# VectorE's two half steps of one tile, declared independent across its two PSUM banks

## The chip, the cores and the metric

One core of a Trainium2 chip runs the kernel. The metric is the time of one execution on the device, in microseconds; lower is better. The profiles are those of single executions, taken by the hardware profiler.

## What is computed

A channel attention feeds a rational feed-forward layer. The attention works on the 256 channels: its scores are 256 by 256 for each of the 4 batches, summed over 6080 rows.

```python
def _attn_ref(q, k, v, tau):                      # (4, 6080, 256) each
    qn = q / (np.linalg.norm(q, axis=1, keepdims=True) + 1e-06)
    kn = k / (np.linalg.norm(k, axis=1, keepdims=True) + 1e-06)
    s = kn.transpose(0, 2, 1) @ qn / tau
    a = softmax(s)                                # over the last axis
    return v @ a

def _moe_ref(x, w_in, w_out, a, b):               # x: (24320, 256), w_in: (256, 2048)
    h = x @ w_in
    P = a[0] + a[1] * h + a[2] * h * h + a[3] * h ** 3
    Q = 1.0 + abs(b[0]) * abs(h) + abs(b[1]) * h * h
    return (P / (Q + 1e-06)) @ w_out
```

## The kernel before

The softmax matrix of a batch is multiplied into w_in once (`fuse`, in 8 parts), so that the main work of a batch is two matmuls with the rational function between them. The 6080 rows of a batch are 12 groups, 11 of 512 rows and one of 448; a group has 8 pairs, each for 256 of the 2048 hidden channels. That makes 48 groups and 384 pairs. Every float32 operand of the large matmuls is held as a high and a low part in TensorE's faster float32 format, and three products stand for one.

What one pair does (`pair`, from line 842), on a PSUM tile `hx` of two banks, one for each 128 channels; x = 0 or 1 is the bank:

- TensorE: `mm1` (line 859), 12 matmuls, 6 into each bank. There are three `hx` tiles, so pair m + 3 needs each bank that pair m frees.
- ScalarE: five activations over both banks at once (lines 886 to 894 and 918): absolute value into `d`, a square into `uu`, a square on `d`, a reciprocal square root from `d` into `r`, and the square of `r`.
- VectorE: the numerator in place in `hx` (line 892), and the quotient's high part into `gh` (line 925), over both banks.
- GpSimd: `d` scaled (line 896), then `d` times the high part, for each bank alone (line 939).
- VectorE, for each bank alone: the remainder in place in `hx[:, x]` (line 941, "rest"), and its product with `r` into `gl[:, x]` (line 945, "last"), the low part of the quotient. In the profile they are `hx<-hx,fast,d` and `gl<-hx,r` of 128x512; the numerator is `hx<-uu,fast,hx`, the quotient `gh<-hx,fast,r`, both 128x1024. In this text: remainder 0 and 1, product 0 and 1.
- TensorE: `out_hi` (8 matmuls on `gh`) and `out_lo` (4 matmuls on `gl`) into the sum `acc` of the group.

Product x is the last reader of its bank, so it is what pair m + 3's matmuls into that bank wait for.

The order on each engine is not left to the compiler. `Planner.order` (line 178) works through all steps with costs and due times (the tables at lines 21 to 50) and gives one list; the steps are issued in that order. `InOrder` (line 69) wraps each engine: behind every instruction it calls `keep_in_program_order` (line 80), which ties the instruction to the one before it on the same engine, and then `apart`. The planner's plan is the same before and after the change.

The dependencies, and with them the waits on semaphores, are found by the framework from the tiles that instructions read and write. `hx` counts as one tile. `apart` (line 335) takes some of these dependencies back: `half[0]` holds, while a step runs, the slot and bank that it uses and its other buffers; `seen` keeps the last 40 instructions of each slot and bank; and `declare_no_dep` says that an instruction needs no dependency on one of another engine that used the other bank and none of the same buffers. Instructions of one and the same engine were left out of it.

The flag `quick` chooses at run time between two bodies of the program; the traces are of the first.

Of the kernel before, what the change touches and what calls it, by code (L numbers as in the profile page):

```python
# [125 lines left out]
def flat(bufs):  # L126
    return [x for b in bufs for x in (b.both if isinstance(b, Pair) else [b])]
# [165 lines left out]
def tile_channel_attention_rational_ffn(  # L293
# [38 lines left out]
    half = [None]  # L332
    seen = {}

    def apart(eng, ins):


        if half[0] is None:
            return
        slot, bank, rest = half[0]  # L340
        for other, old, used in seen.get((slot, 1 - bank), ()):
            if other is not eng and not used & rest:
                tc.declare_no_dep(ins.ins, old.ins, reason="the two use different banks of one tile")
        mine = seen.setdefault((slot, bank), [])
        mine.append((eng, ins, rest))
        del mine[:-40]

    pe = InOrder(tc, nc.tensor, apart)
    dve = InOrder(tc, nc.vector, apart)
    act = InOrder(tc, nc.scalar, apart)  # L350
    pool = InOrder(tc, nc.gpsimd)
    sp = InOrder(tc, nc.sync)
# [15 lines left out]
    def buf(tag, shape, dtype=F32, name=None):  # L368


        def view(slot):
            sizes = dict(zip("abc", shape[1:]))
            t = homes[tag][slot]
            if t.dtype != dtype:
                t = t.bitcast(dtype)
            t = t[:, : math.prod(shape[1:])]
            names = " ".join(sizes)
            return t.rearrange(f"p ({names}) -> p {names}", **sizes) if len(sizes) > 1 else t

        homes.setdefault(tag, 0)  # L380
        homes[tag] = max(homes[tag], math.prod(shape[1:]))
        return Buf(tag, view)
# [75 lines left out]
    def body(quick):  # L458
        lag, when = (LAG, TIME) if quick else (GENERAL_LAG, GENERAL_TIME)
        plan = planner(when)  # L460
        II, T0 = when["pair"], when["start"]
        def step(eng, cost, key, fn, reads=(), writes=(), port=False, rank=None):
            new = [b for b in flat(writes) if b.tag is not None and not b.writers]
            used = {id(b): b for b in (*flat(reads), *flat(writes))}.values()
            own = [b for b in used if b.tag in ("hA", "hB")]
            rest = [b for b in used if b.tag not in ("hA", "hB")]

            def run():
                for b in new:
                    b.tile = b.view(b.slot)  # L470
                at = {(b.slot, b.tag == "hB") for b in own}
                if len(at) == 1:
                    half[0] = *at.pop(), {(b.tag, b.slot) if b.tag else id(b) for b in rest}
                fn()
                half[0] = None

            plan.add(eng, cost, key, run, reads, writes, port, rank)
# [4 lines left out]
        def piece(side, m, at, c):  # L482
# [71 lines left out]
            else:  # L554
                dst, ok = None, w_out_ok[m]
                where = slice(2 * m, 2 * m + 2)
                whi, wlo = (x[:, where].rearrange("p f e -> p (f e)") for x in (w_out_hi, w_out_lo))
            step("SP", 1.45, at, load, (), [raw])
            step("ACT", 0.67, c, rescale, [raw], [kept])
            one, two = (0.45, 0.7) if port else (0.62, 0.7)  # L560
            step("DVE", one, c, low_bits, [kept], [work], port)
            step("DVE", two, c + 0.1, high_bits, [kept, work], [work], port)
            step("DVE", one, c + 0.2, power, [work], [work], port)
# [278 lines left out]
        def pair(m, at, vparts, w, acc):  # L842
# [3 lines left out]
            s = n / 512  # L846
            (vhi, vlo), (whi, wlo) = vparts, w
            hx = banks()
            d, r = buf("d", [P, 2, GT]), buf("r", [P, 2, GT])
            y = buf("uu", [P, 2, GT], F32, "uu")  # L850

            def c(b):
                return b[:, :, :n]

            def due(name):
                x = lag[name]
                return at + (x[p] if isinstance(x, tuple) else x)

            def mm1(i):
                idx = 0  # L860
                for e in range(NC2):
                    for a, x in ((whi, vhi), (whi, vlo), (wlo, vhi)):
                        pe.matmul(
                            hx[:, i, :n], a[:, e, i * P : (i + 1) * P], x[:, e, :n],
                            start=(idx == 0), stop=(idx == 3 * NC2 - 1),
                        )
                        idx += 1

            for i in range(2):
                fn = lambda i=i: mm1(i)  # L870
# [8 lines left out]
                                start=(first and i == parts[0] and a is w[0]), stop=(last and i == 1 and a is w[-1]),  # L879
                            )  # L880

            def put(eng, per, fixed, name, fn, reads, writes, rank=None, later=0.0):
                step(eng, per * s + fixed, due(name) + later, fn, reads, writes, False, None if rank is None else at + rank)

            if quick:
                fn = lambda: act.activation(c(d), c(hx), AF.Abs)
                put("ACT", 0.87, 0.16, "abs", fn, [hx], [d], 1.0)
                fn = lambda: act.activation(c(y), c(hx), AF.Square, bias=half2)
                put("ACT", 0.87, 0.25, "zz", fn, [hx], [y], 1.0)
                fn = lambda: act.activation(c(d), c(d), AF.Square, bias=half1)  # L890
                put("ACT", 0.87, 0.22, "shift", fn, [d], [d])
                fn = lambda: dve.scalar_tensor_tensor(c(hx), c(y), kappa, c(hx), op0=ALU.add, op1=ALU.mult)
                put("DVE", 1.06, 0.23, "num", fn, [y, hx], [hx])
                fn = lambda: act.activation(c(r), c(d), AF.Abs_reciprocal_sqrt, bias=eps)
                put("ACT", 0.87, 0.22, "root", fn, [d], [r], 6.0)
                fn = lambda: pool.tensor_scalar(c(d), c(d), ones[:, 0:1], eps, op0=ALU.mult, op1=ALU.add)
                put("POOL", 1.06, 0.1, "one", fn, [d], [d])
                first = c0
            else:
                kk = buf("uu", [P, 2, GT], F32, "kk")  # L900
                fn = lambda: act.activation(c(kk), c(hx), AF.Abs, scale=b1)
                put("ACT", 0.87, 0.25, "kk", fn, [hx], [kk], 1.0)
                fn = lambda: dve.scalar_tensor_tensor(c(d), c(kk), b0, c(hx), op0=ALU.add, op1=ALU.mult)
                put("DVE", 1.06, 0.22, "prod", fn, [kk, hx], [d], 1.0)
                fn = lambda: act.activation(c(d), c(d), AF.Abs)
                put("ACT", 0.87, 0.2, "absd", fn, [d], [d])
                fn = lambda: act.activation(c(y), c(hx), AF.Identity, scale=a3, bias=a2)
                put("ACT", 0.87, 0.33, "slope", fn, [hx], [y], 1.0)
                fn = lambda: dve.tensor_tensor(c(y), c(y), c(hx), op=ALU.mult)
                put("DVE", 1.06, 0.16, "num1", fn, [y, hx], [y])  # L910
                fn = lambda: dve.scalar_tensor_tensor(c(hx), c(y), a1, c(hx), op0=ALU.add, op1=ALU.mult)
                put("DVE", 1.06, 0.23, "num2", fn, [y, hx], [hx])
                fn = lambda: act.activation(c(r), c(d), AF.Abs_reciprocal_sqrt, bias=ONE)
                put("ACT", 0.87, 0.2, "root", fn, [d], [r], 6.0)
                fn = lambda: pool.tensor_scalar(c(d), c(d), ones[:, 0:1], ONE, op0=ALU.mult, op1=ALU.add)
                put("POOL", 1.06, 0.07, "one", fn, [d], [d])
                first = a0
            fn = lambda: act.activation(c(r), c(r), AF.Square)
# [3 lines left out]
            ghi, glo = buf("gh", [P, 2, GT], F32R), buf("gl", [P, 2, GT], F32R)  # L922
            ghi_ok = Buf()
            t_ok, glo_ok = ([Buf() for _ in range(2)] for _ in range(2))
            fn = lambda: dve.scalar_tensor_tensor(c(ghi), c(hx), first, c(r), op0=ALU.add, op1=ALU.mult)
# [11 lines left out]
            def tail(x):  # L937
                h = hx.both[x]
                fn = lambda: pool.tensor_tensor(d[:, x, :n], d[:, x, :n], ghi[:, x, :n].bitcast(F32), op=ALU.mult)
                put("POOL", 1.16, 0.1, "again", fn, [d, ghi, ghi_ok], [t_ok[x]], later=0.1 * x)  # L940
                fn = lambda: dve.scalar_tensor_tensor(
                    hx[:, x, :n], hx[:, x, :n], first, d[:, x, :n], op0=ALU.add, op1=ALU.subtract
                )
                put("DVE", 0.53, 0.22, "rest", fn, [h, d, t_ok[x]], [h], later=0.1 * x)
                fn = lambda: dve.tensor_tensor(glo[:, x, :n], hx[:, x, :n], r[:, x, :n], op=ALU.mult)
                put("DVE", 0.53, 0.14, "last", fn, [h, r, *([glo] if x else [])], [glo_ok[x], *([] if x else [glo])], 10.0, 0.1 * x)

            for x in range(2):
                tail(x)
                out_hi(x)  # L950
                out_lo(x)
# [70 lines left out]
        for G in range(TG):  # L1022
            b, g = divmod(G, NG)
            at = T0 + G * NFP * II
# [57 lines left out]
```

## Time and profile before

| | |
|---|---|
| median of 3 runs | 2478.53 us (2477.7 to 2479.44) |
| the profiled execution's own time | 2477.43 us |
| its span, first to last instruction | 2475.4 us |
| busy: TensorE, VectorE, ScalarE, GpSimd | 96%, 89%, 88%, 72% |
| granted TensorE clock, mean | 0.987 of full speed |

PE is TensorE (PEld its weight loads), DVE VectorE, ACT ScalarE, POOL GpSimd. Matmuls are pipelined and their ends are modelled: a row's duration reaches past the start of the next. In a timeline a row is: start, duration, engine, line, operation, what it writes and reads, shapes and count; behind it, in brackets, how long the engine had been idle before it and what released it. Neighbours of one kind stand as one row (x2). All instructions have line 79, that of the wrapper.

### The profile page before, as it was taken

Reading aid. Unit: us, or ns where it says so; the run is one execution under the profiler, and the core shown is the slowest. Engines: PE = TensorE matmul, PEld = TensorE weight load, DVE = VectorE, ACT = ScalarE, POOL = GpSimd, SP = SyncE. Lnnn points to the kernel's source line nnn. Section 1 sums busy time; section 2 is a strip of 40 time slices with the busy share of each in tenths; the row PEclk is TensorE's granted clock in tenths of the full one; section 3 lists DMA queues with packets and bytes.
Section 4 is the critical chain, followed back from the end, with each engine's and each line's share of the span. In section 5 each row is a group of like instructions: output and inputs, shape, how many; then the busy total and the mean of one; then the engine's idle time right before and its main releaser. Section 6 shows DMA issues by size and latency. Waiting matters only on the chain.

```text
span 2475.4 us, 30913 instructions
## 1 busy us (share of the span) xinstructions
PE 2375.3 (96%) x10400; PEld 1942.0 (78%) x10400; DVE 2196.5 (89%) x2684; ACT 2169.3 (88%) x2156; POOL 1770.5 (72%) x1353
## 2 busy tenths in 40 slices
PE   5799999999999999999999999999999999999997
PEld 4677777888788877778788888777878777777786
DVE  6879999988978899999987889999997999999996
ACT  3589999978877899999977789999997999999996
POOL 4387777787679877777768986777774777767765
PEclk9799999999999999999999999999999999999999
DMA  8542112252267611211236731112111110100100
GB/s 248 138 113 42 28 18 35 47 131 56 41 147 171 116 24 18 35 18 18 34 69 157 163 58 25 27 18 35 17 18 20 30 19 18 35 18 18 33 9 18
DMA packets 416890, 141.19 MB, mean 57 GB/s; under 512 B 351344, under 2 KB 406064, under 8 KB 416720
## 3 DMA queue, kind: packets, MB, share of 16 engines
q1 hardware_dynamic: 408176, 108.04, 20.2%
q0 software_dynamic: 8544, 31.07, 7.1%
q8 instruction: 84, 1.38, 0.2%
q14 instruction: 86, 0.70, 0.1%
HBM read 83.10 MB, written 24.90 MB: 44 GB/s over the span
## 4 chain that ended last, share of the span: by engine, by line
PE 74%; DVE 12%; issue 5%; ACT 3%; POOL 2%; DMA 2%; SPq 1%; DVEq 0%; POOLq 0%; ACTq 0%
PE hx L79 40%; PE acc L79 34%; DVE hx L79 5%; DVE gl L79 4%; DVE gh L79 2%; POOL d L79 1%; SPq L79 1%; ACT d L79 1%; ACT r L79 1%; DMA kq<-in_q_dram 1%; DVE orow L79 1%; ACT uu L79 1%; DMA d<-in_moe_w_in_dram 1%; ACT L79 0%; DMA r<-in_k_dram 0%
## 5 line engine op out<-in xcount | busy, mean ns | idle before, releaser
L79 POOL TENSOR_TENSOR d<-d,gh 128x512 f32<-128x512 f32 (+1 forms) x768 | 977.9, 1304 | 498.0 <-DVE gh L79 495.2
L79 PE MATMUL hx<-vhi,w 128*128 128x512 f32 (+1 forms) x3072 | 1046.1, 395 | 30.0 <-DVE gl L79 27.6
L79 PEld LDWEIGHTS hx<-vhi,w 128*128 128x128 f32 x3072 | 579.8, 189 | 195.0 <-DVE gl L79 77.0
L79 DVE SCALAR_TENSOR_TENSOR hx<-hx,fast,d 128x512 f32<-128x512 f32 (+1 forms) x768 | 574.7, 748 | 82.3 <-POOL d L79 53.4
L79 PE MATMUL hx<-vlo,w 128*128 128x512 f32 (+1 forms) x1536 | 598.6, 390 | 0.0
L79 DVE TENSOR_TENSOR gl<-hx,r 128x512 fp32r<-128x512 f32 (+1 forms) x768 | 516.9, 681 | 40.3 <-PE acc L79 3.2
L79 POOL TENSOR_SCALAR d<-d,ones,fast 128x1024 f32<-128x1024 f32 (+1 forms) x384 | 470.7, 1226 | 101.0 <-ACT r L79 100.6
L79 ACT ACTIVATE uu<-hx,fast 128x1024 f32<-128x1024 f32 (+1 forms) x384 | 423.1, 1102 | 135.3 <-PE hx L79 122.9
L79 DVE SCALAR_TENSOR_TENSOR hx<-uu,fast,hx 128x1024 f32<-128x1024 f32 (+1 forms) x384 | 487.2, 1269 | 45.3 <-ACT d L79 35.6
L79 DVE SCALAR_TENSOR_TENSOR gh<-hx,fast,r 128x1024 fp32r<-128x1024 f32 (+1 forms) x384 | 485.8, 1265 | 42.1 <-ACT r L79 34.8
L79 PE MATMUL acc<-gh,w_out_hi 128*128 128x512 f32 (+1 forms) x1536 | 476.7, 392 | 3.2 <-DVE gh L79 2.4
L79 PE MATMUL acc<-gl,w_out_hi 128*128 128x512 f32 (+1 forms) x1536 | 473.8, 390 | 4.4 <-DVE gl L79 4.3
L79 PE MATMUL acc<-gh,w_out_lo 128*128 128x512 f32 (+1 forms) x1536 | 470.3, 387 | 0.0
L79 ACT ACTIVATE r<-d,fast 128x1024 f32<-128x1024 f32 (+1 forms) x384 | 439.7, 1145 | 10.9
L79 ACT ACTIVATE d<-d,fast 128x1024 f32<-128x1024 f32 (+1 forms) x384 | 439.4, 1145 | 8.5
L79 ACT ACTIVATE d<-hx 128x1024 f32<-128x1024 f32 (+1 forms) x384 | 386.5, 1007 | 38.2 <-PE hx L79 32.3
L79 ACT ACTIVATE r<-r 128x1024 f32<-128x1024 f32 (+1 forms) x384 | 403.7, 1052 | 9.1
L79 PEld LDWEIGHTS acc<-gh,w_out_hi 128*128 128x128 f32 x1536 | 287.6, 188 | 65.0 <-ACT orow L79 3.3
L79 PEld LDWEIGHTS acc<-gl,w_out_hi 128*128 128x128 f32 x1536 | 287.8, 188 | 62.9 <-DVE gl L79 6.4
L79 PEld LDWEIGHTS acc<-gh,w_out_lo 128*128 128x128 f32 x1536 | 288.6, 188 | 57.8
L79 PEld LDWEIGHTS hx<-vlo,w 128*128 128x128 f32 x1536 | 290.3, 189 | 52.4
L79 PE MATMUL hx<-kq 128*128 128x256 f32 (+1 forms) x592 | 136.7, 385 | 17.8 <-DVE r L79 17.8
(105 smaller groups left out, 1154.8 us busy)
## 6 DMA issues: line engine op xcount, KB each, us to landing
ssq<-sq POOLq DMA_DIRECT2D x54, 512.0 KB, 4.9
out_dram<-orow SPq DMA_DIRECT2D x178, 128.0 KB, 3.2
vst<-in_v_dram SPq DMA_DIRECT2D x176, 128.0 KB, 3.8
kq<-in_k_dram SPq DMA_DIRECT2D x78, 256.0 KB, 4.4
kq<-in_q_dram SPq DMA_DIRECT2D x78, 256.0 KB, 4.8
d<-in_moe_w_in_dram SPq DMA_DIRECT2D x8, 512.0 KB, 6.9
ssq<-sq POOLq DMA_DIRECT2D x6, 448.0 KB, 5.3
r<-in_k_dram SPq DMA_DIRECT2D x10, 256.0 KB, 6.2
```

The lines of the kernel that those rows point to most:

```text
L79: ins = op(*args, **kwargs)
```

## The change

Each step of `rest` and `last` carries a mark `lane`, the pair's number and the bank. In `apart`, two instructions with marks of the same pair and different banks are declared independent of each other even where they are of one engine and use the same other buffers (`r` and `gl` are shared by the two products, each of which uses its own half). Only VectorE has such steps. Nothing else changes: the plan, the instructions and their operands are the same.

```diff
-        slot, bank, rest = half[0]
-        for other, old, used in seen.get((slot, 1 - bank), ()):
-            if other is not eng and not used & rest:
+        slot, bank, rest, lane = half[0]
+        for other, old, used, side in seen.get((slot, 1 - bank), ()):
+            beside = lane is not None and side is not None and lane[0] == side[0] and lane[1] != side[1]
+            if beside or (other is not eng and not used & rest):
                 tc.declare_no_dep(ins.ins, old.ins, reason="the two use different banks of one tile")
         mine = seen.setdefault((slot, bank), [])
-        mine.append((eng, ins, rest))
+        mine.append((eng, ins, rest, lane))
...
-                put("DVE", 0.53, 0.22, "rest", fn, [h, d, t_ok[x]], [h], later=0.1 * x)
+                put("DVE", 0.53, 0.22, "rest", fn, [h, d, t_ok[x]], [h], later=0.1 * x, lane=(m, x))
...
-                put("DVE", 0.53, 0.14, "last", fn, [h, r, *([glo] if x else [])], [glo_ok[x], *([] if x else [glo])], 10.0, 0.1 * x)
+                put("DVE", 0.53, 0.14, "last", fn, [h, r, *([glo] if x else [])], [glo_ok[x], *([] if x else [glo])], 10.0, 0.1 * x, (m, x))
```

`step` and `put` pass `lane` on to `half[0]`.

## Rows read from the trace of the kernel before

**Rows 1.** The page, part 1: busy time, share of the span, instructions.

```profile
PE 2375.3 (96%) x10400; PEld 1942.0 (78%) x10400; DVE 2196.5 (89%) x2684; ACT 2169.3 (88%) x2156; POOL 1770.5 (72%) x1353
```

**Rows 2.** Windows: stretch and length, busy us of PE, PEld, DVE, ACT, POOL.

```profile
268.90:448.50 179.60, 177.44 (x769) 143.22 (x769) 171.76 (x200) 173.17 (x165) 129.52 (x100) 1.00 0.15 24
884.50:1244.60 360.10, 355.30 (x1538) 286.26 (x1537) 344.09 (x401) 346.65 (x329) 258.77 (x200) 1.00 0.15 24
1477.90:1837.60 359.70, 355.16 (x1538) 286.34 (x1537) 344.06 (x402) 346.48 (x329) 258.75 (x200) 1.00 0.15 24
1950.10:2411.10 461.00, 455.29 (x2002) 365.96 (x2001) 423.40 (x491) 445.13 (x431) 323.74 (x250) 1.00 0.12 22
1317.30:1430.10 112.80, 112.80 (x508) 95.20 (x507) 88.57 (x104) 82.75 (x80) 100.12 (x77) 1.00 0.73 159
```

**Rows 3.** Timeline of TensorE: the stall that returns with each group.

```profile
1113.29 0.50 PE L79 MATMUL hx<-vhi,w 128*128 128x512 f32 x1 [0.54 <-DVE gl L79]
...
1158.26 0.50 PE L79 MATMUL hx<-vhi,w 128*128 128x512 f32 x1 [0.57 <-DVE gl L79]
```

**Rows 4.** Waits of the weight loads, whole span: us in total, times, longest.

```profile
PEld hx L79 <- DVE gl L79: 81.2, 139, 3.8
```

**Rows 5.** Timeline of VectorE, one pair of a steady group.

```profile
1137.79 1.28 DVE L79 SCALAR_TENSOR_TENSOR gh<-hx,fast,r 128x1024 fp32r<-128x1024 f32 x1
1138.98 0.68 DVE L79 TENSOR_TENSOR gl<-hx,r 128x512 fp32r<-128x512 f32 x1
1139.58 1.28 DVE L79 SCALAR_TENSOR_TENSOR hx<-uu,fast,hx 128x1024 f32<-128x1024 f32 x1
1140.76 0.75 DVE L79 SCALAR_TENSOR_TENSOR hx<-hx,fast,d 128x512 f32<-128x512 f32 x1
1141.62 0.69 DVE L79 TENSOR_TENSOR gl<-hx,r 128x512 fp32r<-128x512 f32 x1
1142.42 0.76 DVE L79 SCALAR_TENSOR_TENSOR hx<-hx,fast,d 128x512 f32<-128x512 f32 x1
1143.09 1.27 DVE L79 SCALAR_TENSOR_TENSOR gh<-hx,fast,r 128x1024 fp32r<-128x1024 f32 x1
```

**Rows 6.** Timeline of VectorE, other places of the same group.

```profile
1112.54 0.69 DVE L79 TENSOR_TENSOR gl<-hx,r 128x512 fp32r<-128x512 f32 x1
...
1118.03 0.76 DVE L79 SCALAR_TENSOR_TENSOR hx<-hx,fast,d 128x512 f32<-128x512 f32 x1 [0.29 <-POOL d L79]
1118.89 1.29 DVE L79 TENSOR_TENSOR gl<-hx,r 128x512 fp32r<-128x512 f32 x2
...
1124.33 1.27 DVE L79 SCALAR_TENSOR_TENSOR gh<-hx,fast,r 128x1024 fp32r<-128x1024 f32 x1
...
1129.34 1.58 DVE L79 SCALAR_TENSOR_TENSOR hx<-hx,fast,d 128x512 f32<-128x512 f32 x2
```

**Rows 7.** Timeline of ScalarE in the same group.

```profile
1117.74 1.12 ACT L79 ACTIVATE uu<-hx,fast 128x1024 f32<-128x1024 f32 x1 [0.55 <-DVE hx L79]
...
1123.13 1.06 ACT L79 ACTIVATE r<-r 128x1024 f32<-128x1024 f32 x1
```

**Rows 8.** Timeline of GpSimd: both half products of the pair in rows 5.

```profile
1139.21 2.55 POOL L79 TENSOR_TENSOR d<-d,gh 128x512 f32<-128x512 f32 x2
```

**Rows 9.** Timeline of VectorE in a group of the last batch.

```profile
2163.37 1.28 DVE L79 SCALAR_TENSOR_TENSOR gh<-hx,fast,r 128x1024 fp32r<-128x1024 f32 x1 [0.93 <-ACT r L79]
...
2169.27 1.27 DVE L79 SCALAR_TENSOR_TENSOR gh<-hx,fast,r 128x1024 fp32r<-128x1024 f32 x1
...
2172.03 0.76 DVE L79 SCALAR_TENSOR_TENSOR hx<-hx,fast,d 128x512 f32<-128x512 f32 x1 [0.29 <-POOL d L79]
2172.89 0.69 DVE L79 TENSOR_TENSOR gl<-hx,r 128x512 fp32r<-128x512 f32 x1
...
2174.36 1.27 DVE L79 SCALAR_TENSOR_TENSOR gh<-hx,fast,r 128x1024 fp32r<-128x1024 f32 x1
```

**Rows 10.** Timeline of TensorE in the same group of the last batch.

```profile
2140.78 0.50 PE L79 MATMUL hx<-vhi,w 128*128 128x512 f32 x1 [0.55 <-DVE gl L79]
```

More of the change, by code (lines that the diff above doesn't have):

```diff
@@ L461, in body, with step @@
         II, T0 = when["pair"], when["start"]
-        def step(eng, cost, key, fn, reads=(), writes=(), port=False, rank=None):
+        def step(eng, cost, key, fn, reads=(), writes=(), port=False, rank=None, lane=None):
             new = [b for b in flat(writes) if b.tag is not None and not b.writers]
@@ L472, in run @@
                 if len(at) == 1:
-                    half[0] = *at.pop(), {(b.tag, b.slot) if b.tag else id(b) for b in rest}
+                    half[0] = *at.pop(), {(b.tag, b.slot) if b.tag else id(b) for b in rest}, lane
                 fn()
@@ L880, in mm2, with put @@
                             )
-            def put(eng, per, fixed, name, fn, reads, writes, rank=None, later=0.0):
-                step(eng, per * s + fixed, due(name) + later, fn, reads, writes, False, None if rank is None else at + rank)
+            def put(eng, per, fixed, name, fn, reads, writes, rank=None, later=0.0, lane=None):
+                step(eng, per * s + fixed, due(name) + later, fn, reads, writes, False, None if rank is None else at + rank, lane)
             if quick:
```

## The prediction

> **What bounds the kernel now.** I read the page first: TensorE is busy 96% of the span, VectorE 89%, ScalarE 88% [rows 1]. The windows over stretches then show two regimes. Where a batch's scores are being summed, TensorE is busy all of the time and VectorE 88.6 of 112.8 us; what VectorE saves there cannot count [rows 2]. In the long plain stretches three engines are nearly full at once. There the timeline of TensorE repeats: the same stall stands before a first matmul into a freed bank at 1113.29 and at 1158.26, released both times by VectorE's half product [rows 3]. So a group of eight pairs takes 44.97 us, and 179.6, 360.1 and 359.7 us of such time are 20 groups; the last batch has 10 groups in 461.0 us [rows 2]. In a steady group VectorE is busy 43.0 of 45 us and ScalarE 43.3 (344.1 and 346.7 of 360.1, by 8), and TensorE idles 0.6 us, behind VectorE. A stall costs a little more than its idle time, since busy time runs to a matmul's modelled end, past the next one's start. Over the whole span the weight loads wait 81.2 us for the half product [rows 4]: about the ceiling of any gain, 3.3%.
>
> **What a wait costs.** In the timeline of VectorE one pair reads: quotient 1137.79, product 1 of the pair before 1138.98, numerator 1139.58, remainder 0 1140.76, product 0 1141.62, remainder 1 1142.42, next quotient 1143.09 [rows 5]. Start to start, a remainder followed by an independent instruction takes 0.67 (1142.42 to 1143.09), one followed by its own product 0.86 (1140.76 to 1141.62). A product followed by an independent instruction takes 0.60 (1138.98 to 1139.58), product 0 followed by remainder 1 takes 0.80. The instructions themselves last the same. So a wait of VectorE for its own last instruction costs 0.19 to 0.20 us. The first, of product 0 for remainder 0, is real and stays; the second, of remainder 1 for product 0, comes from the shared tile alone, and the change takes it. The same cost stands where the order is remainder 0, remainder 1, product 0: there the second and the third step wait (1118.03 to 1118.89 is 0.86) [rows 6].
> The Trainium skill, VectorE: DVE Perf Modes, section "The DRAIN you can't avoid", speaks against the change: chained VectorE operations take the same time with a semaphore after each as with one after the last. By it the sum would be zero. The steps above do not bear it out for this kernel.
>
> **If the order of instructions stays.** A steady group, 1113.23 to 1158.21, has eight such waits on VectorE's run: five of remainder 1 behind product 0, one of remainder 1 behind remainder 0 (the two at 1129.34 take 1.58 together), two of product 0 behind remainder 1 (the one at 1118.89 among them) [rows 5, 6]. That is 8 x 0.19 = 1.5 us. But VectorE is not the only path: product 0 ends at 1113.23 (1112.54 and 0.69) and frees the bank for TensorE, whose matmuls let ScalarE's square start at 1117.74 (0.55 idle); from there ScalarE runs without a hole to 1124.19, and the quotient that needs its result starts at 1124.33 [rows 3, 6, 7]. Only 0.1 us can go before 1124.33; behind it lie six of the waits, 1.1 us. With ScalarE and TensorE so full I take 0.9 us a group: 20 x 0.9 = 18 us. In the last batch the chain is tied at 2163.37, where the quotient waits 0.93 us for ScalarE, and at 2140.78, where TensorE waits 0.55 for the product [rows 9, 10]; between the two lie four waits: 0.75 x 10 = 7.5 us. For the start and the changes of batch I add 6 (0 to 10). Sum 31.5 us.
>
> **Why I do not expect the order to stay.** Line 80 ties each instruction to the one before it on its engine by an edge of order alone. Between neighbours that edge and the dependency name the same instruction and are one edge, and the declaration takes it whole. So far it was used between engines only, where no such edge is. With the change remainder 1 is no longer tied behind product 0 when the two are neighbours, and the compiler fills a free engine with the first instruction in program order that is ready by its own estimate. When remainder 0 ends, product 0 is not ready (it needs that remainder), and remainder 1 is, if GpSimd's product for it counts as done. GpSimd starts both halves right after the quotient (1139.21, the quotient ends at 1139.07), two VectorE instructions ahead of remainder 0 [rows 5, 8], so an estimate that puts GpSimd a little short calls it ready. I expect remainder 0, remainder 1, product 0 in most pairs that now have remainder 0, product 0, remainder 1. No trace shows this; it is an inference from the code.
>
> **What that order costs.** Take the pair above. GpSimd's two halves run from 1139.21 for 2.55 us, to 1141.76 [rows 8]. Remainder 0 is at 1140.76 as before; remainder 1 could issue at 1141.43 but waits for GpSimd until 1141.79; product 0 follows at 1142.46 without a wait, the next quotient at 1143.06. Against 1143.09 VectorE gains 0.03 us: the wait for GpSimd takes the place of the two waits. But product 0 comes 0.84 us later (1142.46 for 1141.62), and TensorE waits for it, for the bank. Four pairs of a steady group have this form. At 1113.29 and 1158.26 TensorE already waits for exactly such a product [rows 3], so there all of it lands on the path product, TensorE, ScalarE, quotient at 1124.33: 0.84 less 0.10 of slack. Behind that point VectorE still wins 0.19 and 0.12 around 1129.34, 0.19 in a pair that has the numerator between remainder 0 and product 0, and three times 0.03: 0.59. Net 0.84 - 0.10 - 0.59 = +0.15 us a group; 20 groups, +3.0 us.
> In the last batch the pair at 2172.03 loses on VectorE itself: its remainder 0 already waited 0.29 for GpSimd. By the distances of the pair at 1116 to 1120 (remainder 1 behind a GpSimd wait), remainder 1 moves to 2.75 us behind the quotient's end (2170.54), product 0 to 3.42 and the next quotient to 4.02, against 3.82 now (2174.36): +0.20. Its product comes 1.07 later (2173.96 for 2172.89), but the matmul that takes it has the stall of 2140.78, 46.1 us on, behind it: 0.55 idle and some 0.3 for the ends that overlap. Both paths come to about +0.2 [rows 9, 10]. 10 x 0.2 = +2.0 us.
> Elsewhere I take zero: in the stretches of scores TensorE is full [rows 2]. Bounds: if TensorE never came to wait for the late product, VectorE's 0.7 to 0.8 us a group would be won, -16 us; if in two pairs of each group the delay fell to TensorE (1.3 us in a steady group, 1.1 in the last batch), +37 us. I take the path, since its slacks are read off one by one.
>
> **Rivals.** (1) The order stays and the waits go: 2477.4 - 31.5 = 2445.9 for the profiled run, 2447 us for the median. For it: a product's wait is short, 0.1 us of idle engine, and an estimate may round it away. Against it: the one edge. It decides from the point where the estimate has GpSimd's second half end after remainder 0. (2) Product 0 is pushed behind the next quotient as well, 1.19 us more: VectorE fills its hole at remainder 1, but TensorE gets the bank 2.0 us late; by the same path about +1.3 us in steady groups and +1.2 in the last batch, 2477.4 + 38 + 1.1 = 2517 us. For it speaks that nothing ties product 0 to a place any more; against it that it is first in program order and ready by then. (3) The declaration does nothing, or the waits come back in other places: 2478.5 us. Against it stands that the same declaration already works between engines.
>
> **How the numbers follow.** The profiled run took 2477.43 us, 2.0 over its span; the median of the runs is 1.1 above. Forecast, order moved: 2477.43 + 5.0 + 1.1 = 2484 us, own range 2470 to 2500. Chances: moved 0.62 (within it faster by over 0.2% 0.07, within 0.2% 0.25, slower 0.30, as 5 us stand beside errors of 10), rival 1 0.22, rival 2 0.12, rival 3 0.04. Together faster 0.29, same 0.29, slower 0.42. Two tenths of a per cent, 5 us, is about what a measurement of this kernel can tell from no change. The range reaches down to rival 1, 2440, and up to 2505, leaving out most of rival 2 and the tails.
>
> **What would show it.** In a steady group of the changed kernel: remainder 1 directly behind remainder 0 with 0.3 to 0.4 us idle released by GpSimd, product 0 behind it with no gap, and a longer stall of TensorE where it now waits 0.54 to 0.57 us. If instead product 0 still stands between the remainders and remainder 1 starts 0.60 us behind it, the order stayed, and the period should be near 44.1 us. A period of 44.97 with steps of 0.80 means that the declaration does nothing. I am wrong altogether if VectorE's steps get longer, or if the period moves by more than 0.5 us with the order I expect.

## The result, and the profile after

The changed kernel takes 2510.48 us (median of four runs, 2507.77 to 2512.51) against 2478.11 us before: a ratio of 1.0131, 95% interval 1.0113 to 1.0148, so 32 us slower. The forecast was 5 us slower, with an upper end of 2505. The profiled run took 2512.51 us.

The page after, part 1 [rows 1]:

```profile
PE 2372.7 (95%) x10400; PEld 1945.8 (78%) x10400; DVE 2166.9 (86%) x2684; ACT 2170.3 (86%) x2156; POOL 1767.0 (70%) x1353
```

VectorE is busy 30 us less than before, and the span is 35 us longer (2510.5 for 2475.4 us). The work has not grown; the holes have. The waits of the kernel after name them (us in total, times, longest):

```profile
PEld hx L79 <- DVE gl L79: 91.5, 116, 3.5
...
DVE hx L79 <- POOL d L79: 151.9, 300, 4.7
...
PE hx L79 <- DVE gl L79: 50.2, 69, 3.0
PE acc L79 <- DVE sacc L79: 8.0, 1, 8.0
PE hx L79 <- DVE sacc L79: 5.9, 3, 2.6
```

The weight loads wait 91.5 us for the half product, 81.2 before [rows 4]. VectorE's remainders wait 151.9 us for GpSimd; the kernel before has

```profile
DVE hx L79 <- POOL d L79: 53.4, 130, 1.9
...
PE hx L79 <- DVE gl L79: 29.1, 44, 3.4
...
PE acc L79 <- DVE sacc L79: 0.8, 1, 0.8
PE hx L79 <- DVE sacc L79: 0.5, 1, 0.5
```

TensorE's waits for `sacc`, the sum of the scores, were 1.3 us in all and are 13.9 now: the forecast has nothing of the kind.

The windows after, columns as in [rows 2], for a long plain stretch, the last batch and the stretch in which the scores of the fourth batch are summed:

```profile
903.50:1265.50 362.00, 353.41 (x1538) 286.30 (x1536) 340.14 (x402) 346.91 (x329) 258.43 (x201) 1.00 0.15 24
...
1981.70:2445.50 463.80, 452.03 (x2001) 366.19 (x2000) 416.54 (x491) 444.89 (x431) 323.36 (x251) 1.00 0.12 22
1338.40:1457.40 119.00, 115.97 (x506) 96.00 (x507) 86.52 (x104) 82.83 (x80) 98.32 (x77) 0.99 0.67 143
```

The plain stretch grew by 1.9 us and the last batch by 2.8, about the size of the forecast. The stretch of scores grew by 6.2 us, and TensorE, which had no hole there before [rows 2], now idles 3.0 of 119.0 us. That window opens just behind a wait of TensorE:

```profile
1338.38 0.48 PE L79 MATMUL hx<-vhi,w 128*128 128x512 f32 x1 [2.56 <-DVE sacc L79]
```

Counted from the first matmul of that group (1315.74 before, 1334.07 now), the stretch of scores grew by 9.0 us.

A pair of a steady group on VectorE, the one that answers to [rows 5]:

```profile
1168.01 1.27 DVE L79 SCALAR_TENSOR_TENSOR gh<-hx,fast,r 128x1024 fp32r<-128x1024 f32 x1
...
1170.99 0.75 DVE L79 SCALAR_TENSOR_TENSOR hx<-hx,fast,d 128x512 f32<-128x512 f32 x1
1172.03 0.76 DVE L79 SCALAR_TENSOR_TENSOR hx<-hx,fast,d 128x512 f32<-128x512 f32 x1 [0.29 <-POOL d L79]
1172.69 0.68 DVE L79 TENSOR_TENSOR gl<-hx,r 128x512 fp32r<-128x512 f32 x1
1173.29 1.27 DVE L79 SCALAR_TENSOR_TENSOR gh<-hx,fast,r 128x1024 fp32r<-128x1024 f32 x1
```

This is the order that the forecast expected: remainder 1 behind remainder 0 with 0.29 us idle released by GpSimd, product 0 behind it without a gap, quotient to quotient 5.28 us where it was 5.30. TensorE's stall at the end of the group is longer, as expected, and a second one stands two pairs ahead of it [rows 3]:

```profile
1168.15 0.50 PE L79 MATMUL hx<-vhi,w 128*128 128x512 f32 x1 [0.49 <-DVE gl L79]
1178.71 0.50 PE L79 MATMUL hx<-vhi,w 128*128 128x512 f32 x1 [0.74 <-DVE gl L79]
```

I then took the length of each of the 48 groups of eight pairs in both traces, from the first matmul of a group to the first of the next. Steady groups: 44.97 us before, about 45.4 after. But the first group is 7.4 us longer, group 12 (counted from 0) 5.4, group 24 7.8, group 8 2.3. (Group 23 is 2.6 us shorter: a stretch of 3.4 us in which TensorE's granted clock is 0.50 lies in group 23 before, from 1263.56 on, and in group 24 now, from 1339.67 on.) Those are the group at the start and groups in which scores are summed. VectorE's instructions, compared one by one between the two kernels, say what is special there. Beside the swap of neighbours in all 158 pairs that had remainder 0, product 0, remainder 1, there are 41 places, of three to nine instructions, where a remainder 1 went further forward: past a numerator, a quotient, a transpose, remainder 0 of its own pair, or the sum of the scores. I call the first *near swaps* and the second *far moves*. The orders of the four other engines are the same in both kernels. In group 12 of the kernel after VectorE reads

```profile
743.09 1.28 DVE L79 SCALAR_TENSOR_TENSOR gh<-hx,fast,r 128x1024 fp32r<-128x1024 f32 x1
747.59 0.76 DVE L79 SCALAR_TENSOR_TENSOR hx<-hx,fast,d 128x512 f32<-128x512 f32 x1 [3.23 <-POOL d L79]
748.26 0.68 DVE L79 TENSOR_TENSOR sacc<-hx,sacc 128x512 f32<-128x512 f32 x1
748.86 1.27 DVE L79 SCALAR_TENSOR_TENSOR gh<-hx,fast,r 128x1024 fp32r<-128x1024 f32 x1
```

and the same quotient with what follows in the kernel before

```profile
732.16 1.28 DVE L79 SCALAR_TENSOR_TENSOR gh<-hx,fast,r 128x1024 fp32r<-128x1024 f32 x1
734.58 0.69 DVE L79 TENSOR_TENSOR sacc<-hx,sacc 128x512 f32<-128x512 f32 x1 [1.14 <-PE hx L79]
735.44 1.29 DVE L79 SCALAR_TENSOR_TENSOR gh<-hx,fast,r 128x1024 fp32r<-128x1024 f32 x1 [0.17 <-PE acc L79]
736.64 1.62 DVE L79 SCALAR_TENSOR_TENSOR hx<-hx,fast,d 128x512 f32<-128x512 f32 x2
```

In the kernel after remainder 1 stands at VectorE's head and waits 3.23 us for GpSimd; the sum of the scores comes 5.17 us behind the quotient's start instead of 2.42, and TensorE waits 2.31 us for that sum at 748.99:

```profile
748.99 0.67 PE L79 MATMUL hx<-vhi,w 128*128 128x512 f32 x1 [2.31 <-DVE sacc L79]
```

What GpSimd was doing in these 3 us, in the kernel after:

```profile
742.27 0.89 POOL L79 DMA_DIRECT2D ssq<-sq  x1
742.89 2.20 POOL L79 TENSOR_TENSOR sq<-kq 128x1024 f32<-128x1024 f32 x1
744.75 2.81 POOL L79 TENSOR_TENSOR d<-d,gh 128x512 f32<-128x512 f32 x2
```

The half products that the remainder needs stood behind a DMA issue and a square for the next scores, work that GpSimd has only where scores are made. But that is the smaller part: the half products start 0.38 us after the quotient that they need has ended (744.37), and take 2.81 us themselves. In the kernel before, the same DMA issue and square (731.41, 732.03) stand ahead of them too, and nothing waits, since the remainders come only at 736.64. What costs is the new place of the remainder, directly behind its quotient. So the theory after the result: the declaration takes the wait and the order (as predicted); waits gone are a gain, near swaps about undo it (as predicted), and the far moves, which were not predicted, are the loss.

### The profile page after: what moved, and what is told of

It is laid out like the page before. It is cut to its first block, busy times and chain, and to the rows that moved or that the text cites. A ratio compares the mean times of both kernels' runs of the same rounds, so it can differ in the third digit from the quotient of the medians.

```text
span 2510.5 us, 30647 instructions
## 1 busy us (share of the span) xinstructions
PE 2372.7 (95%) x10400; PEld 1945.8 (78%) x10400; DVE 2166.9 (86%) x2684; ACT 2170.3 (86%) x2156; POOL 1767.0 (70%) x1353
## 5 line engine op out<-in xcount | busy, mean ns | idle before, releaser
L79 DVE SCALAR_TENSOR_TENSOR hx<-hx,fast,d 128x512 f32<-128x512 f32 (+1 forms) x768 | 567.4, 746 | 152.3 <-POOL d L79 151.9
L79 PEld LDWEIGHTS acc<-gh,w_out_lo 128*128 128x128 f32 x1536 | 288.6, 188 | 57.9
```

The source lines that it names most:

```text
L79: ins = op(*args, **kwargs)
```

## Experiments

All kernels compute the whole result. The first four ran on one chip beside the kernel before (2477.69 us there), the second four on another (2479.36 us).

**The order alone, put back.** On top of the change, an edge of order without a dependency between a half step and its neighbour on the other bank; it goes by way of an empty instruction (`nop`) on SyncE:

```diff
+ORDER = mybir.DependencyInfo(mybir.DependencyClass.NoSync, mybir.DependencyReason.DATA)
 ...
+            if now is not None and self.was is not None and self.was[1][0] == now[0] and self.was[1][1] != now[1]:
+                tie = self.tc.nc.sync.nop()
+                self.tc.add_manual_dep(tie.ins, self.was[0].ins.name, ORDER, reason="order")
             ins = op(*args, **kwargs)
             self.tc.keep_in_program_order(ins)
+            if tie is not None:
+                self.tc.add_manual_dep(ins.ins, tie.ins.name, ORDER, reason="order")
```

> The change, and on top of it an edge of order alone between a half step on one bank and the half step on the other bank when they are neighbours on VectorE, so that VectorE's order is that of the kernel before and only the waits are gone. Theory A (a wait of VectorE for its own last instruction costs 0.19 us and part of it lies on the path; the order is what costs): 2478 - 31 = 2447 us, a steady group near 44.1 us; the order of the changed kernel then costs about 63 us. Rival B (such waits cost nothing in the end, because VectorE is not the path): 2478 us, and the order costs the 32 us that were measured. Rival C (the loss comes from the declaration itself, not from the order): near 2510 us.

Measured: 2435.96 us, ratio 0.9835 (0.9819 to 0.9852), 42 us faster than before. VectorE's order is that of the kernel before in every instruction. A pair of a steady group:

```profile
1130.60 0.75 DVE L86 SCALAR_TENSOR_TENSOR hx<-hx,fast,d 128x512 f32<-128x512 f32 x1
1131.45 0.69 DVE L86 TENSOR_TENSOR gl<-hx,r 128x512 fp32r<-128x512 f32 x1
1132.06 0.75 DVE L86 SCALAR_TENSOR_TENSOR hx<-hx,fast,d 128x512 f32<-128x512 f32 x1
```

Product 0 to remainder 1 is 0.61 us, 0.80 before [rows 5]; remainder 0 to product 0, a real dependency, is still 0.85. TensorE no longer stalls in a steady group, whose length is 43.9 us, and the stretch that was 360.1 us long [rows 2] has not a hundredth of idle TensorE in it:

```profile
871.10:1222.20 351.10, 351.10 (x1538) 287.01 (x1536) 339.99 (x402) 344.41 (x329) 259.38 (x201) 1.00 0.16 25
```

Theory A holds, with a gain larger than its 31 us; rivals B and C fall. The change loses through the order alone: with the edge put back it is 3% faster than without it. This version beats both kernels.

**Near swaps alone.** The change, with each VectorE instruction also tied to the second to fifth instruction ahead of it:

```diff
+            if self.far is not None:
+                for old in self.far[:-1]:
+                    self.tc.add_manual_dep(ins.ins, old, ORDER, reason="order")
+                self.far = [*self.far, ins.ins.name][-5:]
```

> The change, with each VectorE instruction tied by edges of order to the second to fifth instruction ahead of it, so that an instruction can only change places with its neighbour. Left is remainder 0, remainder 1, product 0 in 158 pairs that have remainder 0, product 0, remainder 1 before; the 41 places where the changed kernel pulls a remainder further ahead (in front of a numerator, a quotient, a transpose or the sum of the scores) are gone. Theory A (the far moves make up the miss of the prediction: 0.4 us a steady group and 0.2 in the last batch from the near swaps, some 25 us from the start and the stretches of scores): 2478 + 10 = 2488 us, a steady group at 45.4 us. Rival B (the near swaps do all of it): 2510 us.

Measured: 2479.71 us, ratio 1.0012 (1.0002 to 1.0022): 44 us above the kernel with the order kept, and 31 below the changed one. Theory A again; the 2488 were a little high. Steady groups are 45.4 us long, as in the changed kernel. With the compiler held to what the forecast assumed, the time is within 5 us of the forecast's 2484.

**Far moves alone.** The edges of the first experiment, and VectorE's steps written in the changed order at the 41 places (each entry: where, and the new order of so many steps):

```diff
+MOVED = "115:374560182 126:34012 139:201 ... 738:3012 745:2301 753:40123 ... 2547:201"
-        return plan.order()
+        return moved(plan.order()) if quick else plan.order()
```

> As the kernel with the order kept, but the 41 places at which the changed kernel pulls remainder 1 further ahead are written in that order; the near swaps are left out. Theory A (a remainder that is pulled ahead waits at the head of VectorE for GpSimd and holds the rest behind it): the time of the kernel with the order kept plus some 25 us, 2472 us if that is 2447, the loss in the first group (7 us) and in the groups 3, 8, 9, 12 to 14, 24 to 26. Rival B (the far moves cost nothing): the same time as with the order kept.

Measured: 2467.22 us, ratio 0.9961 (0.9947 to 0.9975): 31 us above the kernel with the order kept. By the group lengths 11.1 us of it come in group 0, 7.2 in groups 12 to 14, 9.4 in 24 to 26, 3.3 in 8 and 9, 1.8 in 3; group 36 gives 1.4 back. In group 0 the copy of the scores' sum is the victim. VectorE of the changed kernel at that place:

```profile
145.39 0.76 DVE L79 SCALAR_TENSOR_TENSOR hx<-hx,fast,d 128x512 f32<-128x512 f32 x1 [1.49 <-POOL d L79]
147.85 0.76 DVE L79 SCALAR_TENSOR_TENSOR hx<-hx,fast,d 128x512 f32<-128x512 f32 x1 [1.70 <-POOL d L79]
```

and its TensorE:

```profile
151.69 1.22 PE L79 MATMUL acc<-gh,w_out_hi 128*128 128x512 f32 x2 [8.02 <-DVE sacc L79]
```

In the kernel before, that copy stood ahead of the first remainder:

```profile
144.74 0.69 DVE L79 COPY sacc<-acc 128x512 f32<-128x512 f32 x1 [0.53 <-PE acc L79]
```

Now two remainders of two pairs wait for GpSimd ahead of it, it starts at 150.96, and TensorE stands for 8 us. Only half of the 11.1 us in group 0 is idle time of TensorE, though (11.8 us with the far moves, 6.1 with the order kept). The other half is its clock: the mean granted clock in that group is 0.88, against 0.97, and the same 222 matmuls keep it busy for 57.5 us instead of 52.0. (The length of group 0 scatters by up to 2.8 us between kernels that are alike there, so its 11 us are rough.)

**The order moved, the waits kept.** The kernel before with its VectorE steps written in the changed kernel's order, near and far, without the declaration (left out are three pairs of neighbours in the softmax, which also stand the other way round in the changed kernel):

```diff
+MOVED = "115:374560182 126:34012 ..."   # all 194 places
-        return plan.order()
+        return moved(plan.order()) if quick else plan.order()
```

> The kernel before, without the declaration, its VectorE instructions written in the order in which the changed kernel has them (in six places one instruction differs). Only the order changes, each wait of a half step for the one before it is still there. Theory A (waits and order add up: waits gone -31, order +63): 2478 + 63 = 2541 us; bounds 2510 (the waits are all covered by the idle time that the order makes) to 2545. Rival B (the waits cost nothing): 2510 us.

Measured: 2553.12 us, ratio 1.0305 (1.0288 to 1.0322). Outside the bounds that I gave, because the order costs 75 us, not 63. But the waits are worth the same in either order: 2553.1 - 2510.5 = 42.6 us here, 41.7 with the order kept. The three parts add up: -42 for the waits, +44 near, +31 far, together +33; the change measured +32. The waits of VectorE for GpSimd and of the weight loads for the product say it as well, order kept, near and far:

```profile
PEld hx L86 <- DVE gl L86: 36.0, 81, 2.9
...
DVE hx L86 <- POOL d L86: 49.9, 126, 2.0
```

```profile
PEld hx L81 <- DVE gl L81: 83.9, 108, 3.5
...
DVE hx L81 <- POOL d L81: 105.7, 280, 2.2
```

```profile
PEld hx L92 <- DVE gl L92: 42.0, 83, 3.2
...
DVE hx L92 <- POOL d L92: 97.5, 149, 4.7
...
PE hx L92 <- DVE sacc L92: 6.0, 3, 2.6
```

The near swaps make many short waits for GpSimd (280) and a late product; the far moves make few more waits (149 against 126), but long ones, and delay the sums.

**One far move.** The order kept, and a single one of VectorE's 2574 steps moved, the remainder of group 12 shown above:

```diff
+MOVED = "738:3012"
```

> Waits gone and order kept (2436 us), and one of VectorE's 2574 steps moved: in the first group of the third batch remainder 1 stands ahead of the sum of the scores, of a quotient and of remainder 0, as in the changed kernel. Theory A (VectorE takes its instructions in order, so what stands at its head and waits for GpSimd holds everything behind it): an idle time of 3.3 us behind GpSimd ahead of that remainder, a stall of TensorE of 2.3 us for the sum of the scores, that group longer by 2 to 4 us, the run by as much. Rival B (a stretch in which TensorE is full gives a delay of VectorE back): the group and the run as without the move.

Measured: one run of 2440.45 us, too little to tell 4 us by; the group lengths tell it. Group 12 is 62.1 us long, 57.9 with the order kept: 4.2 us, as much as the far moves together cost in that group. No other length near it moves, and nothing is given back behind it. VectorE, TensorE, and a window on TensorE's clock (the 0.50 in it is the granted clock):

```profile
727.86 0.76 DVE L89 SCALAR_TENSOR_TENSOR hx<-hx,fast,d 128x512 f32<-128x512 f32 x1 [3.22 <-POOL d L89]
728.53 0.68 DVE L89 TENSOR_TENSOR sacc<-hx,sacc 128x512 f32<-128x512 f32 x1
...
736.32 1.12 DVE L89 STREAM_TRANSPOSE orow<-acc 128x896 f32<-128x896 f32 x1 [3.26 <-PE acc L89]
```

```profile
729.27 0.50 PE L89 MATMUL hx<-vhi,w 128*128 128x512 f32 x1 [2.30 <-DVE sacc L89]
...
732.78 0.63 PE L89 MATMUL hx<-vlo,w 128*128 128x512 f32 x1
733.21 0.63 PE L89 MATMUL hx<-vhi,w 128*128 128x512 f32 x1
```

```profile
730.34:733.75 3.41, 3.41 (x10) 2.65 (x9) 2.69 (x5) 0.00 (x0) 3.19 (x3) 0.50 0.83 162
```

TensorE stalls 2.30 us for the sum, its only stall in this group. That is little more than half of the 4.2 us. Behind the stall its granted clock falls to 0.50 for 3.4 us, the lower of its two levels (1.2 instead of 2.4 GHz), and its matmuls start 0.43 us apart instead of 0.23 (729.60 to 729.83): about 1.6 us more. With the order kept TensorE has no stall in this group and the clock stays at 1.00. A transpose on VectorE, which needs TensorE's late result, then waits 3.26 us in its turn, but TensorE does not stall for it. That the far moves together cost the same 4.2 us in this group is chance: there the first stall (2.34 us) leaves the clock at 1.00, and a second one of 1.07 us follows. Theory A, a little above its upper end; it had no term for the clock.

**Which near swap costs.** Swaps in two of the four pairs, in 16 steady groups: in the fifth and seventh pair of a group, then in the fourth and sixth.

```diff
+MOVED = "340:10 352:10 390:10 ..."   # 32 places
```

> Waits gone and order kept (2436 us), and in 16 steady groups the order remainder 0, remainder 1, product 0 in two of the four pairs that the compiler swaps: the fifth and the seventh pair of the group, behind which TensorE stalled for product 0 (0.48 and 0.71 us) when all four were swapped. Theory A (the late product costs where TensorE waits for it, and the prediction counted one such place where there are two): a steady group from 43.9 to 45.1 us, 16 x 1.15 = 18 us, 2454 us, with both stalls. Rival B (VectorE's own wait for GpSimd, the same in each swapped pair, is the cost): half of the 1.45 us, 0.7 a group, 2447 us.

> As the kernel with swaps in the fifth and seventh pair, but in the fourth and sixth. Theory A: no stall of TensorE; VectorE loses 0.16 us in each (it gains 0.03 by a swap against the order with the wait, and 0.19 by the wait that is gone without a swap): 0.3 us a group, 16 x 0.3 = 5 us, 2441 us. Rival B (the same cost in each swapped pair): 0.7 a group, 2447 us.

Measured: 2446.87 and 2443.24 us, ratios 0.9871 (0.9853 to 0.9888) and 0.9860 (0.9842 to 0.9878), against 0.9835 with the order kept: about 9 and 6 us. The group lengths are sharper: in groups with swaps in the group ahead too, +0.93 us for the fifth and seventh pair, +0.46 for the fourth and sixth, 1.48 for all four. Neither theory fits both: rival B has the first time, 2447 us, but expected the same of the second. The pairs ahead of the stalls do cost twice as much, but the others are not the 0.3 of theory A, and a stall of TensorE of 0.5 us at the end of the group is there in both kernels; of the second stall 0.14 us are left in the first kernel and nothing in the other. One reason why the fourth and sixth pair cost more than 0.3 us is seen in the fourth, on VectorE of that kernel:

```profile
1127.46 0.76 DVE L91 SCALAR_TENSOR_TENSOR hx<-hx,fast,d 128x512 f32<-128x512 f32 x1
1128.71 0.76 DVE L91 SCALAR_TENSOR_TENSOR hx<-hx,fast,d 128x512 f32<-128x512 f32 x1 [0.50 <-POOL d L91]
```

and on its GpSimd:

```profile
1123.75 2.41 POOL L91 TENSOR_TENSOR vlo<-orow,vhi 128x1024 fp32r<-128x1024 f32 x1 [0.22 <-ACT vhi L91]
1126.12 2.56 POOL L91 TENSOR_TENSOR d<-d,gh 128x512 f32<-128x512 f32 x2
```

Here GpSimd has other work, `vlo`, for which it waited 0.22 us for ScalarE; its half products run to 1128.68, and remainder 1 waits 0.50 us for them, not the 0.29 of the other pairs.

**The opposite of the near swaps.** Product 0 ahead of remainder 1 in the 111 pairs that have remainder 0, remainder 1, product 0 in the kernel before, waits gone:

```diff
+MOVED = "..."   # 111 entries of the form "n:10"
```

> Waits gone, and the opposite of the near swaps: in the 111 pairs that have remainder 0, remainder 1, product 0 in the kernel before, product 0 goes ahead of remainder 1. Theory A (an early product is worth more than VectorE's time where TensorE waits for it; in steady groups VectorE is the bound once the waits are gone, and there the wait of product 0 for its remainder, 0.19 us in two pairs of a group, less what was idle anyway, counts): steady groups +0.1 to +0.3 us, stretches of scores and last batch 0 to -0.3 a group, together 2434 to 2442 us. Rival B (the planned order of these pairs is worth as much as that of the others): +0.5 us a group, 2455 us or more.

Measured: 2436.41 us, ratio 0.9829 (0.9810 to 0.9848): no difference from the order kept (0.9835). Within theory A's range; rival B falls. An early product is worth nothing that these times could tell where TensorE no longer waits for it.

## Why the prediction went wrong, point by point

Group lengths in us against the kernel before, by the stretches of the forecast's sum (20 steady groups, 10 of the last batch, the 18 others), each from one profile:

| | steady, 20 | last, 10 | others, 18 |
|---|---|---|---|
| waits gone, order kept: forecast | -18 | -7.5 | -6 |
| measured | -21.1 | -7.6 | -14.3 |
| with near swaps: forecast | +3 | +2 | 0 |
| measured | +5.9 | +2.5 | -7.6 |
| the change as it is (near and far): measured | +7.1 | +2.8 | +25.5 |

**The price of a wait** was right: 0.80 became 0.61 us when the wait went, and the waits as a whole are worth 42 us in either order. The rule of the Trainium skill that was weighed there (VectorE: DVE Perf Modes, section "The DRAIN you can't avoid"), by which semaphores between chained operations add nothing, is not borne out here: with it the first experiment would have shown 2478 us, not 2436.

**The gain if the order stays** (rival 1) was right in the last batch and near in the steady groups (1.05 us a group for 0.9). The term for start and changes of batch, 6 us with an upper bound of 10, was too small: 14.3.

**That the order does not stay** was right, and for the reason given: with the edge of order put back and nothing else, the old order is back in every instruction. All 158 pairs with remainder 1 behind product 0 were swapped.

**The cost of that order** was right in direction and place, and small against the miss: 2480 us measured with near swaps only, 2484 forecast. In the steady groups it came to +0.3 us a group instead of +0.15. The path was as drawn (product late, TensorE's stall from 0.57 to 0.74, a later square): from the quotient ahead of the stall to the one at its end it takes 16.33 us with near swaps (1105.35 to 1121.68) and 15.62 before (1108.71 to 1124.33), 0.71 more where the forecast had 0.74. What VectorE wins behind it was sized too high, 0.59 us. In the kernel with near swaps the six quotients of a group from 1121.68 on stand 6.90, 6.02, 5.62, 5.28 and 5.28 us apart, and 7.24, 6.22, 5.30, 5.29 and 5.30 before: a win of 0.25. The failing one is the third, 5.62 for 5.30: VectorE, 0.54 us ahead by then, runs into GpSimd's `vlo`, which did not come earlier.

**The step that failed** is "Elsewhere I take zero: in the stretches of scores TensorE is full". Two things are wrong with it. I read the missing tie for one kind of pair only, remainder 1 next to product 0. It is missing wherever remainder 1 follows a half step on the other bank, and once remainder 1 is free on that side it can pass everything ahead of it that is not ready by the compiler's estimate, other pairs' steps and the scores' sum included. And a full TensorE was taken as cover. It is full because VectorE hands it the sums in time: in group 12, where TensorE has no idle time with the order kept, one remainder that waits 3.2 us at VectorE's head made it stall 2.3 us, its clock fell behind the stall, and the group became 4.2 us longer. The far moves cost 31 us in the experiment and 35 in the change (against near swaps alone, by group lengths), and they are the whole difference between 2480 and 2510. Of the 31, 20 lie in the groups in which scores are summed and 11 in group 0. There TensorE was not full even before (it idled 6 us), so for that part of the zero the forecast gave no reason at all. TensorE's clock, which the forecast left out as well, is half of those 11.

Rival 2, product 0 behind the next quotient, gave 2517 us and would have been near in time; it did not happen, as the pair shown above has product 0 ahead of the quotient. Rival 3 is out. That the compiler counts GpSimd's half products as done too early is an inference still: the traces show that the remainders it pulled forward wait for GpSimd, and how long its half products take, but not what the compiler reckoned with.

## What to carry to other kernels

A false dependency between neighbours on one engine may be the only thing that keeps them in order: when it is declared away, put an edge of order in its place, and compare the order of instructions before comparing times. Here the same declaration is 32 us slower alone and 42 us faster with that edge. On an engine that takes its instructions in order, an instruction that is free to move should never stand ahead of work that other engines wait for, unless its own inputs come early; an engine that is always busy is no cover for a delay of the one that feeds it.

## What was not expected of the hardware

The waits of VectorE for its own last instruction cost the same in two very different orders, 41.7 and 42.6 us, though VectorE idles 50 us for GpSimd in one and 147 in the other; parts of the schedule add up within 2 us where I had expected them to cover each other. And a delay need not fade: a single step, moved ahead of three others and 0.7 us long itself, made its group 4.2 us longer, more than the 3.2 us that it waited. TensorE stood 2.3 us and then ran 3.4 us at half its clock. That is not so behind each such stall: in the same group of the kernel with all far moves the clock stayed at 1.00 behind one of 2.34 us.
